# Attention into a gated feed-forward layer on one core: three early gate/value blocks, casts in another place, merged squares, and two output tiles moved forward

## The chip, the core and the metric

The kernel runs on one core of a Trainium2 chip. The core has TensorE (PE: matmuls, and PEld: its weight loads), VectorE (DVE), ScalarE (ACT), GpSimd (POOL) and SyncE (SP), each with an instruction stream of its own that it works through in order. DMA transfers are issued from SP's and GpSimd's streams and run on 16 shared DMA engines. The metric is the device time of one execution in microseconds; lower is better.

## What is computed

```python
# q, k, v: 8 batches, 12 heads, 448 rows, 64 columns
scores = q @ k.T / sqrt(64)
attn   = max(scores, 0) ** 2 / 448
x      = attn @ v                      # -> 3584 tokens x 768
xn     = x / sqrt(mean(x * x) + 1e-6) * rms_g
g, val = xn @ w_gate, xn @ w_val       # 768 -> 1536
out    = (g * sigmoid(g) * val) @ w_out    # 1536 -> 768
```

Inputs and output are float32; the kernel works in bfloat16 with float32 sums.

## The kernel before

The work is done batch by batch, with the tokens of a batch (448) along the free axis. A head pair j (0 to 5) fills 128 partitions; the six pairs of a batch are the six slices of 128 of the 768 model columns.

**Attention** of batch b (lines 136 to 241). For batches 0 and 1 TensorE transposes q and k (`pe_transposes`, L142) and VectorE copies the result out (`qkT`, L148). From batch 2 on VectorE reorders q and k (`kqp`, L155) and a DMA transposes them (`kqT`, L166). `scores` (L187) makes score tiles psS for two of four chunks of rows at a time; there are two buffers of psS. The relu leaves psS by ScalarE (L196) or, for the chunks named by `dve_chunks`, by VectorE (L194). `squares` (L202) multiplies r by itself on VectorE, one instruction for each chunk. `attend` (L209) multiplies by v into psAV, of which there is one buffer. ScalarE writes xT from it (L220), and VectorE x*x, `x2` (L221).

**Norm.** `norm_stat` sums x2 over the columns with a matrix of ones (psSS, L251), ScalarE takes the root (L258), VectorE the reciprocal (L262, rstd). `norm_apply` forms xn = xT * g * rstd in six VectorE instructions (L268).

**Feed-forward.** `gate` and `value` make one block of 128 of the 1536 hidden columns each: twelve matmuls into psG or psV (L251; each is one half of 64 output partitions). ScalarE takes the silu of psG (L289), VectorE multiplies it with psV into hT (L295). `outproj` makes an output tile of 128 tokens in two parts, 512 and 256 wide (psO, L251), which ScalarE (L312) and VectorE (L314) copy out; a DMA from SP stores them (L321). psG, psV, psO, psSS and psT share three buffers, `mm`.

**Weights** are loaded in 18 slices of float32 by DMAs from SP into seven staging buffers (`fetch_w`, L115), and GpSimd casts each to bfloat16 (`cast_w`, L125). The first fetch waits for batch 0's last load of k. q, k and v are loaded by GpSimd's casting DMAs (`load`, L95); q and k have one buffer, v has two.

**The order** is fixed by hand: instructions stand in each engine's stream as the program emits them. `spread` takes a main list of units with costs (gate/value blocks, output tiles) and places other units (attention of the next batch, its norm, preparations) at shares of the main cost. In the prologue, batch 0's attention runs alone, with filler matmuls (`warm`, L368) between its units, then its norm, fourteen fillers, and xn. Then gate/value 0 runs; attention 1 begins at 0.45 of it, and what is left of attention 1 stands alone behind it, then the norm of batch 1. The loop over b from 1 (L440) has as its main list gate/value b and out tiles: all seven tiles of batches 0 and 1 at b = 1, three tiles at each even b, four at each odd one from 3 on. Beside it stand attention b + 1, then its `norm_stat` at 0.86 and `norm_apply` at 0.90 of the main cost.

## Time and profile before

| | us |
|---|---|
| median of three runs | 517.49 (513.65 to 518.02) |
| the profiled execution, its own time | 515.89 |
| its span, first to last instruction | 514.10 |
| TensorE busy in the span | 476.3 (93%), mean granted clock 0.963 |
| VectorE busy | 301.0 (59%) |
| ScalarE busy | 256.2 (50%) |
| GpSimd busy | 53.8 (10%) |

All times in the rows below are microseconds from the span's start unless marked ns. A matmul's busy time contains a latency that the next one overlaps, so a unit's cost on TensorE is read as the distance between starts. "Granted clock" is the share of TensorE's full 2.4 GHz; its two levels are 1.2 and 2.4 GHz. The wait in brackets behind an instruction is the idle time of its engine ahead of it and what ended it.

### The profile page before, as it was taken

How to read it: one execution, taken by the hardware profiler on the slowest of the kernel's cores; microseconds unless marked ns; L12 is line 12 of the kernel's file. 1: busy time of each engine (PE TensorE's matmuls, PEld its weight loads, DVE VectorE, ACT ScalarE, POOL GpSimd, SP SyncE). 2: the span in 40 equal slices, each digit the busy share in tenths (PEclk: the TensorE clock that was granted, in tenths of full speed). 3: DMA queues.
4: the chain of work that ended last, by engine and by line, in shares of the span. 5: the costliest groups of instructions: out<-in, count | busy, mean ns of one | idle time of the engine just before them, and what ended most of it. 6: DMA issues, size and time to landing. Idle time of an engine off the chain costs nothing.

```text
span 514.1 us, 10918 instructions
## 1 busy us (share of the span) xinstructions
PE 476.3 (93%) x4754; PEld 264.8 (52%) x4754; DVE 301.0 (59%) x489; ACT 256.2 (50%) x367; POOL 53.8 (10%) x53
## 2 busy tenths in 40 slices
PE   6966899769799999999999999999999999999996
PEld 2322465327545554456554645465555645466774
DVE  2996458953285467576566476756567466545210
ACT  3652146632366466655666466636655556642210
POOL 5283540200200000010001000020000000000000
PEclk8887799959999999999999999999999999999999
DMA  9999920660999751099105930296005210012013
GB/s 116 288 319 258 337 111 2 79 83 1 139 203 132 144 108 34 1 161 171 32 2 92 220 84 1 48 191 124 2 9 108 68 50 1 1 33 62 1 32 93
DMA packets 81712, 50.65 MB, mean 99 GB/s; under 512 B 35072, under 2 KB 76544, under 8 KB 81664
## 3 DMA queue, kind: packets, MB, share of 16 engines
q1 hardware_dynamic: 48944, 33.43, 25.9%
q0 software_dynamic: 32720, 16.52, 25.1%
q8 instruction: 37, 0.61, 0.5%
q14 instruction: 11, 0.09, 0.1%
HBM read 47.19 MB, written 11.01 MB: 113 GB/s over the span
## 4 chain that ended last, share of the span: by engine, by line
PE 76%; DVE 14%; issue 5%; ACT 3%; DMA 1%; POOL 0%; DVEq 0%; ACTq 0%; POOLq 0%
PE psV L251 22%; PE psG L251 22%; PE psO L251 16%; PE psS L187 8%; PE psAV L209 6%; DVE xn L268 5%; DVE r L202 5%; DVE rstd L262 2%; PE psSS L251 2%; DVE r L194 1%; ACT r L196 1%; DMA kb<-in_k_dram 1%; PE psT L142 1%; PE psW L368 1%; ACT xT L220 1%
## 5 line engine op out<-in xcount | busy, mean ns | idle before, releaser
L196 ACT ACTIVATE r<-psS 112x896 bf16<-112x896 f32 x162 | 140.6, 915 | 39.7 <-PE psS L187 39.4
L251 PE MATMUL psG<-xn,wg_sb 128*64 128x448 bf16 x1152 | 136.6, 360 | 13.5 <-DVE xn L268 13.3
L251 PE MATMUL psV<-xn,wv_sb 128*64 128x448 bf16 x1152 | 128.3, 357 | 0.0
L295 DVE TENSOR_TENSOR hT<-sil,psV 128x448 bf16<-128x448 bf16 x96 | 59.6, 621 | 104.0 <-PE psV L251 102.3
L202 DVE TENSOR_TENSOR r<-r 112x896 bf16<-112x896 bf16 x192 | 117.9, 657 | 0.0
L251 PE MATMUL psO<-wo_sb,hT 128*64 128x512 bf16 (+1 forms) x1344 | 115.4, 326 | 0.0
L289 ACT ACTIVATE sil<-psG 128x448 bf16<-128x448 f32 x96 | 52.2, 544 | 104.5 <-PE psG L251 103.2
L251 PEld LDWEIGHTS <-wg_sb 128*64 128x64 bf16 x1152 | 67.8, 110 | 70.1 <-issue 34.9
L251 PEld LDWEIGHTS <-hT 128*64 128x64 bf16 x1344 | 77.9, 110 | 33.6 <-issue 4.0
L251 PEld LDWEIGHTS <-wv_sb 128*64 128x64 bf16 x1152 | 67.5, 111 | 47.2 <-issue 12.8
L209 PE MATMUL psAV<-r,vb 112*64 112x448 bf16 x384 | 49.6, 362 | 7.5 <-DVE r L202 6.5
L220 ACT ACTIVATE xT<-psAV 128x448 bf16<-128x448 f32 x48 | 26.1, 543 | 43.0 <-PE psAV L209 42.6
L312 ACT COPY ost<-psO 128x512 f32<-128x512 f32 x28 | 16.4, 585 | 60.5 <-PE psO L251 56.0
L187 PE MATMUL psS<-kqT 64*128 64x448 bf16 x288 | 40.8, 354 | 3.0 <-ACT r L196 1.5
L221 DVE TENSOR_TENSOR x<-xT 128x448 bf16<-128x448 bf16 x48 | 19.2, 401 | 40.5 <-ACT xT L220 40.4
L262 DVE RECIPROCAL rstd<-rstd 128x448 f32<-128x448 f32 x8 | 23.6, 2953 | 31.7 <-ACT rstd L258 31.7
L209 PEld LDWEIGHTS <-vb 112*64 112x64 bf16 x384 | 22.6, 110 | 28.9 <-issue 13.3
L194 DVE TENSOR_SCALAR r<-psS 112x896 bf16<-112x896 f32 x30 | 32.6, 1086 | 7.1 <-PE psS L187 7.1
L95 POOL DMA_DIRECT2D qb<-in_q_dram x10 | 8.8, 880 | 213.1 <-DVE x L221 135.6
L268 DVE SCALAR_TENSOR_TENSOR xn<-xT,g_sb,rstd 128x448 bf16<-128x448 bf16 x48 | 30.4, 702 | 0.1
L187 PEld LDWEIGHTS <-kqT 64*128 64x128 bf16 x288 | 8.8, 94 | 28.6 <-issue 28.5
L187 PE MATMUL psS<-qkT 64*128 64x448 bf16 x96 | 16.4, 392 | 5.6 <-ACT r L196 3.3
(33 smaller groups left out, 166.3 us busy)
## 6 DMA issues: line engine op xcount, KB each, us to landing
qb<-in_q_dram POOLq DMA_DIRECT2D x7, 672.0 KB, 9.8
kb<-in_k_dram POOLq DMA_DIRECT2D x7, 672.0 KB, 14.8
vb<-in_v_dram POOLq DMA_DIRECT2D x7, 672.0 KB, 10.0
wst<-in_moe_w_gate_dram SPq DMA_DIRECT2D x6, 768.0 KB, 10.7
wst<-in_moe_w_val_dram SPq DMA_DIRECT2D x6, 768.0 KB, 11.7
wst<-in_moe_w_out_dram SPq DMA_DIRECT2D x6, 768.0 KB, 15.8
out_dram<-ost SPq DMA_DIRECT2D x8, 336.0 KB, 3.7
out_dram<-ost SPq DMA_DIRECT2D x8, 288.0 KB, 2.7
```

The costliest lines, as they stand in the source:

```text
L187: nc.tensor.matmul(out=psS[:, hh, :S], lhsT=flat[:, o : o + P], rhs=rhs, start=True, stop=True)
L194: nc.vector.tensor_relu(out=r[:], in_=psS[:PC, :, :S])
L196: nc.scalar.activation(out=r[:], in_=psS[:PC, :, :S], func=ACT.Relu)
L202: nc.vector.tensor_tensor(out=r[:], in0=r[:], in1=r[:], op=ALU.mult)
L209: nc.tensor.matmul(out=psAV[hh * D : (hh + 1) * D, :], lhsT=ld["v", b][:, 2 * j + hh, c * D : (c + 1) * D], rhs=rsq[b, j, c][:, hh, :], st ...
L220: nc.scalar.mul(out=xT[:, j, :], in_=psAV[:], mul=inv_attn)
L221: nc.vector.tensor_tensor(out=x2s[b][:, j, :], in0=xT[:, j, :], in1=xT[:, j, :], op=ALU.mult)
L251: nc.tensor.matmul(out=ps[prt, :w], lhsT=lhsT[:, prt], rhs=rhs, start=start, stop=stop)
L262: nc.vector.reciprocal(out=rstd[:], in_=rstd[:])
L268: nc.vector.scalar_tensor_tensor(out=xn[:, kt, :], in0=xTs[b][:, kt, :], scalar=g_sb[:, kt : kt + 1], in1=rstds[b][:], op0=ALU.mult, op1=A ...
L289: nc.scalar.activation(out=s[:], in_=psG[:], func=ACT.Silu)
L295: nc.vector.tensor_tensor(out=hTs[b // 2][:, fb, o : o + S], in0=sil.pop((b, fb))[:], in1=psV[:], op=ALU.mult)
```

## The change

- **Early blocks.** For batch 0, the gate and value products of hidden blocks 0, 1 and 2 are made from xT, which now holds x*g, without the norm (`early_matmuls`). When rstd is there, VectorE multiplies both products by it as they leave PSUM, and silu and product follow (`early_rest`). Block 0 stands ahead of psSS and blocks 1 and 2 behind it. Blocks 0 and 1 lie in the two psS buffers, block 2 in psAV's and one of `mm`. The fourteen fillers go.
- **g moves.** `leave` multiplies by g and the attention's scale when ScalarE reads psAV; `norm_apply` is a plain product. x*x is now made by ScalarE from psAV.
- **Merged squares.** One tile r holds both chunks of a step, one VectorE instruction squares them; the last pair of batch 0 is split between ScalarE and VectorE. The first two qkT copies of batch 1 go to ScalarE.
- **Attention's order.** `attend` and `leave` come later behind their scores (`lag`).
- **Weights.** The first four slices (two of gate, two of value) are loaded by GpSimd's casting DMAs straight into bfloat16. Fourteen are staged in six buffers; the first of these fetches waits for the last casting DMA. The first two casts stand behind batch 1's loads, which are now in halves and ahead of the early blocks; the other twelve wait for the scaled block 1 of batch 0.
- **Places.** Two output tiles stand behind gate/value 0, five are left at b = 1. Attention 1 is spread over 0.08 to 0.68 of that list, its norm stands at 0.74 and 0.80 of it. In later batches the attention ends at 0.74 instead of 0.80, and the norm stands at 0.80 and 0.84 instead of 0.86 and 0.90. Batch 2's loads and preparation move forward.

The diff, cut to its core:

```diff
-        nc.gpsimd.tensor_copy(out=dst, in_=src)
+        return eng.tensor_copy(out=dst, in_=src)
...
     def scores(b, j, cs, on_dve):
...
-        for c, psS in zip(cs, pss):
-            r = apool.tile([PC, 2, S], BF16, name="r", tag="r")
+        r = apool.tile([PC, len(cs), 2, S], BF16, name="r", tag="r")
...
     def squares(b, j, cs, split=False):
+        r = raw.pop((b, j, cs[0]))
+        if split:
+            nc.scalar.activation(out=r[:, 0], in_=r[:, 0], func=ACT.Square)
+            nc.vector.tensor_tensor(out=r[:, 1], in0=r[:, 1], in1=r[:, 1], op=ALU.mult)
+        else:
             nc.vector.tensor_tensor(out=r[:], in0=r[:], in1=r[:], op=ALU.mult)
...
-        nc.scalar.mul(out=xT[:, j, :], in_=psAV[:], mul=inv_attn)
-        nc.vector.tensor_tensor(out=x2s[b][:, j, :], in0=xT[:, j, :], in1=xT[:, j, :], op=ALU.mult)
+    def leave(b, j):
+        psAV = psAVs.pop((b, j))
+        nc.scalar.mul(out=xTs[b][:, j, :], in_=psAV[:], mul=ga_sb[:, j : j + 1])
+        nc.scalar.activation(
+            out=x2s[b][:, j, :], in_=psAV[:], func=ACT.Square, scale=inv_attn
+        )
...
-            nc.vector.scalar_tensor_tensor(
-                out=xn[:, kt, :], in0=xTs[b][:, kt, :], scalar=g_sb[:, kt : kt + 1],
-                in1=rstds[b][:], op0=ALU.mult, op1=ALU.mult,
+            nc.vector.tensor_tensor(
+                out=xn[:, kt, :], in0=xTs[b][:, kt, :], in1=rstds[b][:], op=ALU.mult
             )
...
+    def early_rest(b, fb, parts):
+        t = late["early"].tile([P, 2, S], FP32, name="gv", tag="gv")
+        for part in range(2):
+            nc.vector.tensor_tensor(
+                out=t[:, part, :], in0=parts[part][:, :S], in1=rstds[b][:], op=ALU.mult
+            )
+        s = spool.tile([P, S], BF16, name="sil", tag="sil")
+        nc.scalar.activation(out=s[:], in_=t[:, 0, :], func=ACT.Silu)
+        hT, o = hidden(b)
+        return nc.vector.tensor_tensor(
+            out=hT[:, fb, o : o + S], in0=s[:], in1=t[:, 1, :], op=ALU.mult
+        )
...
+        for which, s in order[:NCAST]:
+            w, w_sb = ((moe_w_gate, wg_sb) if which == "g" else (moe_w_val, wv_sb))
+            last = nc.gpsimd.dma_start(
+                out=w_sb[:, :, s * FS : (s + 1) * FS],
+                in_=w.rearrange("(kt p) f -> p kt f", p=P)[:, :, s * FS : (s + 1) * FS],
+            )
+        order = order[NCAST:]
         first = fetch_w(*order[0])
+        hold(first, last, "fetches follow what the first batch needs")
...
-        norm_stat(0)
-        warm(14)
-        norm_apply(0)
+        early_matmuls(0, 0, blocks[0])
+        norm_stat(0)
+        psE = ps_a.tile([P, S], FP32, name="psE", tag="ps_a")
+        blocks.append((psE[:], ps_m.tile([P, 512], FP32, name="psE", tag="mm")[:]))
+        early_matmuls(0, 1, blocks[1])
+        early_matmuls(0, 2, blocks[2])
+        ahead(2)
+        norm_apply(0)
+        early_rest(0, 2, blocks[2])
...
+                if fed[0] == 2:
+                    hold(i, held[0], "casts on Pool follow the norm of the first batch")
...
-        for fn in spread(main, [(0.45, 1.3, attention(1, True, lambda j: (3,)))]):
+        main = [(c, stepped(n, f)) for n, (c, f) in enumerate(gate_value(0, 3) + out_tiles(0, 0, 2))]
+        spans = [(0.02, 0.06, [lambda: rest_of(0), lambda: rest_of(1)])]
+        spans.append((0.08, 0.68, pending))
...
-            spans.append((0.0, 0.80, attention(b + 1, False, lambda j: (3,) if j % 2 else ())))
+            spans.append((0.0, 0.74, attention(b + 1, False, lambda j: (3,) if j % 2 else (), True)))
         if b + 1 < B:
-            spans.append((0.86, 0.9, [lambda b=b: norm_stat(b + 1)]))
-            spans.append((0.90, 0.95, [lambda b=b: norm_apply(b + 1)]))
+            spans.append((0.80, 0.82, [lambda b=b: norm_stat(b + 1)]))
+            spans.append((0.84, 0.86, [lambda b=b: norm_apply(b + 1)]))
```

How this moves instructions is shown at three places. First, VectorE at the norm of batch 0. Before (r are squares, x_274 is x*x, then reciprocal, xn, the products into hT):

```order
L221 TENSOR_TENSOR x_274<-xT 128x448
L202 TENSOR_TENSOR r<-r 112x896 x2
L221 TENSOR_TENSOR x_274<-xT 128x448
L262 RECIPROCAL rstd<-rstd 128x448
L268 SCALAR_TENSOR_TENSOR xn<-xT,g_sb,rstd 128x448 x6
L295 TENSOR_TENSOR hT<-sil,psV 128x448 x5
```

VectorE at the same place now (psE is an early block in PSUM, gv the scaled block):

```order
L216 TENSOR_TENSOR r<-r 112x1792
L214 TENSOR_TENSOR r<-r 112x896
L297 RECIPROCAL rstd<-rstd 128x448
L303 TENSOR_TENSOR xn<-xT,rstd 128x448 x6
L328 TENSOR_TENSOR gv<-psE,rstd 128x448 x2
L334 TENSOR_TENSOR hT<-sil,gv 128x448
```

The products x*x are gone from VectorE, the squares are merged, and three scaled blocks (the last two rows stand there three times in a row) come behind xn.

Second, GpSimd at the end of batch 0's loads. Before (wst is a staged slice):

```order
L95 DMA qb<-in_q_dram 112x6x256
L95 DMA kb<-in_k_dram 112x6x256
L95 DMA vb<-in_v_dram 112x6x256
L125 CAST wg_sb<-wst 128x6x256
L125 CAST wv_sb<-wst 128x6x256
```

GpSimd at the same place now:

```order
L100 DMA vb<-in_v_dram 112x6x256
L454 DMA wg_sb<-in_moe_w_gate_dram 128x6x256
L454 DMA wv_sb<-in_moe_w_val_dram 128x6x256
...
L100 DMA qb<-in_q_dram 112x6x256
L100 DMA kb<-in_k_dram 112x6x256
...
L133 CAST wg_sb<-wst 128x6x256
L133 CAST wv_sb<-wst 128x6x256
```

Casting DMAs of four slices and six loads of batch 1 now stand ahead of the first cast.

Third, VectorE at the norm of batch 1. Before:

```order
L202 TENSOR_TENSOR r<-r 112x896 x2
L221 TENSOR_TENSOR x_954<-xT 128x448
L262 RECIPROCAL rstd<-rstd 128x448
L268 SCALAR_TENSOR_TENSOR xn<-xT,g_sb,rstd 128x448 x6
L295 TENSOR_TENSOR hT<-sil,psV 128x448 x6
```

VectorE at the same place now (ost is an output tile, kqp the reordered k of batch 2):

```order
L216 TENSOR_TENSOR r<-r 112x1792
L355 TENSOR_TENSOR hT<-sil,psV 128x448
L297 RECIPROCAL rstd<-rstd 128x448
L303 TENSOR_TENSOR xn<-xT,rstd 128x448 x6
L374 COPY ost<-psO 128x256 x2
L166 COPY kqp<-kb 112x6x4x64
```

The last block of gate/value 0 now stands between the attention of batch 1 and its norm, and the copies of two output tiles and the preparation of batch 2 follow xn.

## Rows read from the trace of the kernel before

**Rows 1.** Stretches: length, busy time (and count) of each engine, clock, DMA share, GB/s

```profile
92.70:114.20 21.50, 13.82 (x92) 5.30 (x90) 17.60 (x28) 10.42 (x14) 2.79 (x3) 0.70 0.74 97
187.00:465.00 278.00, 272.89 (x2800) 148.78 (x2797) 174.73 (x296) 162.13 (x232) 8.38 (x9) 1.00 0.37 68
```

**Rows 2.** Timeline, TensorE, around the first norm: start, length, operation, count, wait

```profile
42.14 1.12 PE L209 MATMUL psAV<-r,vb 112*64 112x448 bf16 x4 [0.25 <-DVE r L202]
...
56.03 2.50 PE L251 MATMUL psV<-xn,wv_sb 128*64 128x448 bf16 x12
```

**Rows 3.** Timeline, VectorE, first attention (last row: a pair of squares in the second)

```profile
11.48 1.09 DVE L194 TENSOR_SCALAR r<-psS 112x896 bf16<-112x896 f32 x1 [1.10 <-PE psS L187]
...
14.97 0.62 DVE L148 COPY qkT<-psT 128x896 bf16<-128x896 bf16 x1 [0.26 <-PE psT L142]
...
19.46 0.62 DVE L148 COPY qkT<-psT 128x896 bf16<-128x896 bf16 x1
...
97.31 1.15 DVE L202 TENSOR_TENSOR r<-r 112x896 bf16<-112x896 bf16 x2
```

**Rows 4.** Timeline, a square on VectorE and two casts on GpSimd beside it

```profile
34.25 3.29 DVE L202 TENSOR_TENSOR r<-r 112x896 bf16<-112x896 bf16 x1
...
33.77 1.88 POOL L125 CAST wv_sb<-wst 128x1536 bf16<-128x1536 f32 x1
35.60 1.46 POOL L125 CAST wg_sb<-wst 128x1536 bf16<-128x1536 f32 x1
```

**Rows 5.** Timeline, TensorE: units whose starts follow each other without a wait

```profile
71.73 0.39 PE L142 MATMUL psT<-ident,kb 112*64 112x112 bf16 x8
...
72.15 1.30 PE L251 MATMUL psG<-xn,wg_sb 128*64 128x448 bf16 x12
73.39 0.55 PE L187 MATMUL psS<-qkT 64*128 64x448 bf16 x4
...
119.07 1.32 PE L251 MATMUL psV<-xn,wv_sb 128*64 128x448 bf16 x12
120.20 1.32 PE L251 MATMUL psG<-xn,wg_sb 128*64 128x448 bf16 x12
...
148.84 0.93 PE L209 MATMUL psAV<-r,vb 112*64 112x448 bf16 x8
149.70 0.55 PE L187 MATMUL psS<-kqT 64*128 64x448 bf16 x4
150.18 1.50 PE L251 MATMUL psO<-wo_sb,hT 128*64 128x256 bf16 x24
...
493.53 15.79 PE L251 MATMUL psO<-wo_sb,hT 128*64 128x512 bf16 x192
```

**Rows 6.** Timeline, TensorE and VectorE, at the boundary to batch 2

```profile
180.33 1.33 PE L251 MATMUL psSS<-x,ones_bf 128*64 128x448 bf16 x12
...
186.16 3.67 DVE L268 SCALAR_TENSOR_TENSOR xn<-xT,g_sb,rstd 128x448 bf16<-128x448 bf16 x6
...
187.28 0.59 PE L251 MATMUL psG<-xn,wg_sb 128*64 128x448 bf16 x4
...
190.19 0.55 PE L187 MATMUL psS<-kqT 64*128 64x448 bf16 x4
```

**Rows 7.** Groups by line: count, busy us, mean ns of one, idle before

```profile
L196 ACT ACTIVATE r<-psS 112x896 bf16<-112x896 f32 x162 | 140.6, 915 | 39.7 <-PE psS L187 39.4
L220 ACT ACTIVATE xT<-psAV 128x448 bf16<-128x448 f32 x48 | 26.1, 543 | 43.0 <-PE psAV L209 42.6
L262 DVE RECIPROCAL rstd<-rstd 128x448 f32<-128x448 f32 x8 | 23.6, 2953 | 31.7 <-ACT rstd L258 31.7
```

**Rows 8.** Loads: first fetch (SP), a cast and its wait (GpSimd), landing of q, k, v

```profile
15.30 0.40 SPq L115 DMA_DIRECT2D wst<-in_moe_w_gate_dram  x1
...
47.70 1.47 POOL L125 CAST wv_sb<-wst 128x1536 bf16<-128x1536 f32 x1 [3.14 <-DMA wst<-in_moe_w_val_dram]
...
DMA to landing us min/median/max: 3.0/9.8/31.9
```

More of the change, by code (lines that the diff above doesn't have):

```diff
@@ L91, in alloc_ld, with fetch @@
         ld["v", b] = ldpool.tile([PC, H, NCH * D], BF16, name="vb", tag="vb", bufs=2)
+    def fetch(b):
+        alloc_ld(b)
+        for nm in ("q", "k", "v"):
+            load(nm, b)
     def load(nm, b, h0=0, h1=H):
@@ L115, in fetch_w, with cast_w @@
         return nc.sync.dma_start(out=dst, in_=src)
-    def cast_w(which, s):
+    def cast_w(which, s, eng=None):
+        eng = eng or nc.gpsimd
         st = stage.pop((which, s))
@@ L124, in cast_w @@
             dst = {"g": wg_sb, "v": wv_sb}[which][:, :, s * FS : (s + 1) * FS]
-        nc.gpsimd.tensor_copy(out=dst, in_=src)
+        if eng is nc.scalar:
+            return nc.scalar.copy(out=dst, in_=src)
+        return eng.tensor_copy(out=dst, in_=src)
     xTs, x2s = {}, {}
@@ L131 @@
     rsq = {}
-    raw = {}
+    raw, psAVs = {}, {}
     HH = H // 2
@@ L147, in pe_transposes @@
         t = late["qkT"].tile([P, 2, S], BF16, name="qkT", tag="qkT")
-        nc.vector.tensor_copy(out=t[:], in_=psT[:])
+        if b == 1 and j < 2:
+            nc.scalar.copy(out=t[:], in_=psT[:])
+        else:
+            nc.vector.tensor_copy(out=t[:], in_=psT[:])
         qkT[b, j] = t
@@ L267, in norm_apply, with hidden, early_matmuls @@
         for kt in range(KT):
-            nc.vector.scalar_tensor_tensor(
-                out=xn[:, kt, :], in0=xTs[b][:, kt, :], scalar=g_sb[:, kt : kt + 1],
-                in1=rstds[b][:], op0=ALU.mult, op1=ALU.mult,
+            nc.vector.tensor_tensor(
+                out=xn[:, kt, :], in0=xTs[b][:, kt, :], in1=rstds[b][:], op=ALU.mult
             )
         xns[b] = xn
+    def hidden(b):
         i = b // 2
-        if b % 2 == 0:
+        if i not in hTs:
             hp = hpool if i % 2 == 0 else late["hpool"]
             hTs[i] = hp.tile([P, FT, 2 * S], BF16, name="hT", tag="hT")
+        return hTs[i], (b % 2) * S
+    def early_matmuls(b, fb, parts):
+        for part, w_sb in enumerate((wg_sb, wv_sb)):
+            for kt in range(KT):
+                halves(
+                    parts[part], S, w_sb[:, kt, fb * P : (fb + 1) * P], xTs[b][:, kt, :],
+                    kt == 0, kt == KT - 1,
+                )
[11 more added lines that the diff above has]
+        )
     def project(w_sb, b, fb, nm):
@@ L324, in outproj, with gate_value @@
                 g += n
-    def gate_value(b):
+    def gate_value(b, f0=0):
         units = []
-        for fb in range(FT):
+        for fb in range(f0, FT):
             units.append((1.13, lambda fb=fb: gate(b, fb)))
@@ L356 @@
     nc.sync.dma_start(out=g_sb[:], in_=moe_rms_g.rearrange("(kt p) -> p kt", p=P))
+    ga_sb = wpool.tile([P, KT], FP32, name="ga_sb", tag="rmsga")
+    nc.vector.tensor_scalar_mul(out=ga_sb[:], in0=g_sb[:], scalar1=inv_attn)
     load("q", 0, 2, 6)
@@ L364, in warm, with hold @@
     def warm(n):
-        ps = ps_a.tile([P, S], FP32, name="psW", tag="ps_a")
+        ps = ps_m.tile([P, S], FP32, name="psW", tag="mm")
         for _ in range(n):
             nc.tensor.matmul(out=ps[:], lhsT=warm_in[:, :P], rhs=warm_in[:], start=True, stop=True)
-    def name_of(i):
-        return (i.ins if hasattr(i, "ins") else i)
-    with tc.tile_pool(name="stage", bufs=7) as sp, tc.tile_pool(name="qkT", bufs=2) as tp:
-        late["stage"], late["qkT"] = sp, tp
+    def hold(i, until, reason):
+        i, until = (x.ins if hasattr(x, "ins") else x for x in (i, until))
+        tc.add_manual_dep(
+            i,
+            until.name,
+            mybir.DependencyInfo(mybir.DependencyClass.Sync, mybir.DependencyReason.DATA),
+            reason=reason,
+        )
+    NST = 6
+    with tc.tile_pool(name="stage", bufs=NST) as sp, tc.tile_pool(name="qkT", bufs=2) as tp, tc.tile_pool(
+        name="early", bufs=2
+    ) as ep:
+        late["stage"], late["qkT"], late["early"] = sp, tp, ep
         order = []
@@ L392 @@
                 warm(2)
-        norm_stat(0)
-        warm(14)
-        norm_apply(0)
+        alloc_ld(1)
+        for h0 in (0, HH):
+            for nm in ("q", "k", "v"):
+                load(nm, 1, h0, h0 + HH)
         fed = [0]
@@ L431, in prepare @@
         dma_transposes(b, half)
-    def fetch(b):
-        alloc_ld(b)
-        for nm in ("q", "k", "v"):
-            load(nm, b)
-    fetch(2)
     full = S // P
```

104 lines of the change are left out of this document (59 added, 45 removed).

## The prediction

> **What bounds the kernel now.** I read the table of stretches first. From 187 us to 465 us TensorE is busy 272.89 of 278.00 us at a granted clock of 1.00, the upper level of 2.4 GHz: nothing but fewer matmuls would help there. Around the second norm (92.70 to 114.20) the clock is 0.70 on average and TensorE is busy 13.82 of 21.50 us [rows 1]. So the time to win lies ahead of 187 us.
>
> Next, TensorE's timeline: the attention of batch 0 ends at 42.14 + 1.12 = 43.26 us, and the second product of gate/value 0 starts only at 56.03, and its twelve matmuls take 2.50 us [rows 2]. Then the time of one unit when nothing is in the way, as the distance from one start to the next [rows 5]: a gate or value block 120.20 - 119.07 = 1.13 us, the sixteen transposes of a head pair 72.15 - 71.73 = 0.42, one psS step 150.18 - 149.70 = 0.48, one psAV 149.70 - 148.84 = 0.86, an out tile 15.6 / 4 = 3.9 (the last 192 matmuls, less 0.2 of latency).
>
> With these I count the work from 43.26 to the first gate of batch 2 at 187.28 [rows 6]: 48 gate and value blocks 54.5; three psSS 3.4 (as many matmuls as a block); six transposes 2.5; two attentions (24 psS, 12 psAV) 21.8; seven out tiles 27.3; one psS of the next batch 0.5. Sum 110.0. The stretch took 144.0, so **34.0 us are lost** in it, and the 43.26 ahead of it are themselves mostly waiting. Last, each batch boundary: the gate starts at 187.28 and is through at 190.19, when psS follows, 2.9 for 1.13 of work: 1.8 lost because six xn products (3.67) still run [rows 6].
>
> **The first attention.** Its pace is VectorE's. Between two copies of qkT lie 19.46 - 14.97 = 4.49 us, with 0.62 for the copy and 1.09 for the relu [rows 3]. Later a square that is half of a 1.15 us pair in the quiet [rows 3] takes 3.29, from 34.25 to 37.54, across two casts on GpSimd that run from 33.77 to 37.06 [rows 4]: 1.36 us for each cast. The change takes the x*x product to ScalarE, merges two squares into one, and removes the casts from this stretch: four weight slices now come as casting DMAs, the next two casts stand behind batch 1's loads, the other twelve behind the norm. VectorE's round becomes copy 0.54 (0.08 of each operation overlaps the next) + relu 1.00 + two merged squares. A merged square isn't in the trace; it lies between 0.9 and the pair's 1.15; I take 1.08. Sum 3.7. ScalarE's round: three relus of 0.9 and two readings of psAV at 0.54 [rows 7], 3.7 as well. The relu of head pair 0 ends at 11.48 + 1.09 = 12.57 [rows 3]. From there four rounds of 3.7 and one of 3.2 (no copy) bring pair 5's relu to 30.6, with its squares, the release of psAV and the last psAV 33.5. Six loads of batch 1 are now issued on GpSimd in this stretch, and a cast may fall on the last squares: 0 to 4 more, I take 1. **The attention ends at 34.5 instead of 43.26: 8.8 won** (5.8 to 9.8).
>
> The Trainium skill ("SBUF — State Buffer", Who interferes with whom) says that a VectorE instruction with two SBUF inputs contends with a GpSimd instruction that reads SBUF, and that the later one fully blocks. The trace agrees: the square on record ends 0.48 us after the second cast, 1.36 us late for each of the two. By that rule each of the twelve casts still to come can cost a square that it meets its whole 1.46 us [rows 4].
>
> **The norm of batch 0.** Call the end of the attention t. Before, only 14 filler matmuls lay between psSS and the first gate. Now block 0 stands ahead of psSS, blocks 1 and 2 behind it. The clock had fallen there before (2.50 us for twelve matmuls where 1.3 is usual [rows 2, 5]), so I let block 0 and psSS take 5.4 instead of 3.4. psSS ends at t + 5.8. Root and reciprocal took 186.16 - 181.46 = 4.7 at a boundary [rows 6], a table load included that isn't needed here; the reciprocal alone is 2.95 [rows 7]; I take 3.7, to t + 9.5; blocks 1 and 2 and a transpose end at t + 10.8. Six xn products at 0.6 (3.67 for six [rows 6]; the new form has one operand fewer, 0.40 to 0.70) end at t + 13.1, and gate/value 3 at t + 14.5. Now comes a new wait: the scores of batch 1 need the two psS buffers that hold blocks 0 and 1 until VectorE has scaled them. VectorE does block 2 first (three products, 1.8), then 0 and 1. None of these products is in the trace; at xn's 0.6 each the second buffer is free at t + 17.9. TensorE reaches t + 18.3 with 11.2 us of work done: **7.1 lost** (5 to 9). Behind the waiting psS stand gate 4 and all that follows.
>
> **Gate/value 0 with attention 1.** 17.0 of blocks and 12.6 of attention, 29.6 for TensorE. VectorE needs 3.7 a round for six rounds, which end 22 us after t + 18.5 if left alone. The held casts run right here: twelve at 0 to 1.36 are 0 to 16 us, where about 7 are free. ScalarE has 3.5 relus, two psAV readings and 1.7 silu a round, 4.9 of the 5.0 that TensorE leaves. I take **5.0 lost** (0 to 11).
>
> **The end of gate/value 0.** The norm of batch 1 has two out tiles beside it instead of nothing. Behind psSS stand one 256-wide part and one whole tile, 5.3 us; the chain from psSS to the last xn took 186.16 + 3.67 - 181.46 = 8.4 at a boundary [rows 6], and the copy of a 256-wide part now stands behind xn in VectorE's queue. **3.1 lost** (2 to 4). Another 2.5 (1.8 to 4) for the change between psS and block matmuls (a block behind a psS takes 1.24 where 72.15 starts one [rows 5], not 1.13), and the first psS of batch 2. Batch 2's kqp copies stand in VectorE's queue right after: its loads are issued when the last cast is through (twelve from 52.5 us on at 1.5 to 1.9 each: about 75 us), some 20 us ahead of their use at 34.5 + 60; hidden, unless they land as late as batch 1's v did, 31.9 us after issue [rows 8].
>
> **Six boundaries.** psSS moves to 0.80 of the main work: two out tiles, 7.8, lie behind it instead of 5.3. The chain of 8.4 is nearly covered, but a 256-wide copy behind xn holds a bank. 1.3 of the 1.8 go: **7.8 won** (4 to 10). The other side: 0.54 of ScalarE for each of 48 x*x [rows 7], 26 us in all, beside TensorE in the later batches; attention in 0.74 of the main work instead of 0.80. I charge **1.5** (0 to 4).
>
> **The sum** is made against the profiled execution, 515.9 us (span 514.1 and 1.8 around it), 1.6 below the median of the runs, 517.5. Stalls now 7.1 + 5.0 + 3.1 + 2.5 = 17.7 against 34.0: 16.3 won. 8.8 + 16.3 + 7.8 - 1.5 = 31.4, which gives **484.5 us**.
>
> **The rivals.**
> (a) Everything hides: attention ends at 33.5 (9.8 won), stalls 5 + 0 + 3.1 + 1.8 = 9.9 (24.1 won), boundaries 1.7 each (10.2). 44.1 in all: 472. For it: VectorE's own work leaves 7 us for the casts. Against: ScalarE is full at the same time.
> (b) The casts are not held back but moved onto attention 1's squares: 12 at 1.36 is 16.3, 9 over what is free, and with a cast on the first attention's tail and a missed kqp copy 3 + 2 more beyond what I counted: 484.5 + 4 + 5 = 494. By the Trainium skill's rule above ("SBUF — State Buffer", Who interferes with whom) it would be 12 x 0.10 = 1.2 us more. For it: both engines have that work in the same 25 us. Against: most of VectorE's other work reads PSUM, and casts can slip in beside it.
> (c) The data come late. Before, the fetches start when 1680 KB of the first batch (as written, in bfloat16) have landed, at 15.30 [rows 8]: 120 KB a us. Behind these now stand the last v and four slices, 1872 KB, to 31 us; only then fetches and batch 1 share the DMA engines, at 1.47 + 3.14 = 4.6 us a slice [rows 8]. Batch 1's first q and k halves then land at about 41; TensorE wants them at t + 10.4 = 45. Should they take as long as the v, to 55, TensorE waits 10: 494.5.
> (d) Slower than before: the clock. If the waits at t + 15 to t + 18 drop TensorE to 1.2 GHz and VectorE-paced work never lets it recover until the norm of batch 1, the 40 us of work in gate/value 0 cost 40 more: 524.5. It decides from 38 us of such work on. For it: 0.70 in the second row of [rows 1]. Against: that row has TensorE busy for 64%, while this stretch would have over 80%.
>
> **How the numbers follow.** Forecast 0.50, (a) 0.17, (b) 0.18, (c) 0.10, (d) 0.03, and 0.02 for a gain that is lost in several small ways and ends near zero. A measurement of this kernel can tell about 1%, 5.2 us, from no change. Faster by more: 0.95, within 0.02, slower 0.03. The range reaches from (a) to a little past (b) and (c): 472 to 499.
>
> **What would show it.** Right: copies of qkT 3.7 us apart in the first attention and psAV's end at 33 to 37 us; psSS of batch 0 between two early blocks and the reciprocal hidden beside them; a wait of psS for VectorE's product on psE; squares of 1.1 that stretch to 2 or 3 beside casts at 52 to 75; gates at the boundaries at 1.2 to 1.6. Wrong: qkT copies still 4.5 apart; early blocks that wait for a DMA; a granted clock of 0.5 beyond 60 us; waits of psS for ScalarE in the later batches.

## The result, and the profile after

| | before | after |
|---|---|---|
| median of four runs each, us | 516.98 (513.65 to 518.02) | 487.12 (486.24 to 488.83) |
| ratio, 95% interval | | 0.9435 (0.9392 to 0.9478) |
| profiled execution, its span | 515.89, 514.1 | 487.15, 485.4 |
| mean granted clock | 0.963 | 0.987 |

The forecast was 484.5 us, range 472 to 499. The change brings 28.7 us of span. Medians and ratios below leave out executions that were disturbed as a whole; the profiles of experiments 4 and 8 (494.58 and 498.80 us) are of such executions, so only single stretches of them are compared.

The table of stretches of after (columns as in [rows 1]), cut near the end of the first attention, the first score of batch 1, the first output tile, gate/value 1 and batch 2:

```profile
37.00:53.00 16.00, 12.80 (x133) 7.10 (x134) 11.20 (x16) 6.36 (x11) 0.00 (x0) 1.00 1.24 258
53.00:90.00 37.00, 33.96 (x366) 18.00 (x364) 27.59 (x28) 27.97 (x42) 24.92 (x15) 0.95 0.89 224
90.00:102.00 12.00, 11.22 (x123) 7.43 (x120) 7.39 (x10) 4.62 (x7) 0.00 (x0) 1.00 0.10 14
166.00:320.00 154.00, 152.80 (x1570) 85.97 (x1570) 88.76 (x116) 100.18 (x152) 8.40 (x9) 1.00 0.50 83
```

The stretch around the second norm, 0.70 of the clock and 64% busy in [rows 1], is now 94% busy (11.22 of 12.00) at 1.00, and from 166 to 320 us TensorE is busy 152.80 of 154.00. TensorE's timeline of after, at the points by which the prediction reckons:

```profile
35.44 1.21 PE L224 MATMUL psAV<-r,vb 112*64 112x448 bf16 x8 [1.31 <-ACT x L240]
...
48.79 1.32 PE L286 MATMUL psV<-xn,wv_sb 128*64 128x448 bf16 x12 [0.69 <-DVE gv L328]
50.59 0.37 PE L198 MATMUL psS<-qkT 64*128 64x448 bf16 x2 [0.48 <-DVE gv L328]
...
52.39 0.37 PE L198 MATMUL psS<-qkT 64*128 64x448 bf16 x2 [1.44 <-DVE gv L328]
52.69 1.92 PE L286 MATMUL psG<-xn,wg_sb 128*64 128x448 bf16 x12
...
89.81 2.78 PE L286 MATMUL psO<-wo_sb,hT 128*64 128x512 bf16 x24
...
98.86 0.38 PE L286 MATMUL psG<-xn,wg_sb 128*64 128x448 bf16 x2
...
101.88 1.33 PE L286 MATMUL psV<-xn,wv_sb 128*64 128x448 bf16 x12
...
115.84 0.55 PE L198 MATMUL psS<-kqT 64*128 64x448 bf16 x4 [1.28 <-issue]
...
142.69 0.95 PE L224 MATMUL psAV<-r,vb 112*64 112x448 bf16 x8 [1.16 <-ACT x L240]
...
149.79 0.95 PE L224 MATMUL psAV<-r,vb 112*64 112x448 bf16 x8 [1.65 <-ACT x L240]
...
166.10 1.33 PE L286 MATMUL psG<-xn,wg_sb 128*64 128x448 bf16 x12
```

The attention of batch 0 ends at t = 35.44 + 1.21 = 36.65 (43.26 in [rows 2]). The gate of batch 2 starts at 166.10 (187.28 in [rows 6]), one whole block without a wait. Between the two lie 129.45 us for the same 110.0 of work that the prediction counts: 19.5 lost, 34.0 before. So the 28.7 us are 6.6 ahead of t, 14.5 from t to 166.10, and 7.5 behind (319.3 us to the span's end instead of 326.8). The new wait is there too: three waits for VectorE's scaled blocks (gv), 0.69, 0.48 and 1.44.

VectorE's timeline of after: three copies of qkT, the last relu and the last half square of the first attention, the six xn, then squares in gate/value 0, beside casts (58.37 to 74.58) and without (last):

```profile
14.88 0.62 DVE L159 COPY qkT<-psT 128x896 bf16<-128x896 bf16 x1 [0.40 <-PE psT L150]
...
18.75 0.62 DVE L159 COPY qkT<-psT 128x896 bf16<-128x896 bf16 x1
...
23.12 0.62 DVE L159 COPY qkT<-psT 128x896 bf16<-128x896 bf16 x1 [0.42 <-PE psT L150]
...
32.14 1.09 DVE L205 TENSOR_SCALAR r<-psS 112x896 bf16<-112x896 f32 x1 [0.93 <-PE psS L198]
...
34.34 1.88 DVE L214 TENSOR_TENSOR r<-r 112x896 bf16<-112x896 bf16 x1
...
44.36 3.30 DVE L303 TENSOR_TENSOR xn<-xT,rstd 128x448 bf16<-128x448 bf16 x6
...
58.37 3.74 DVE L216 TENSOR_TENSOR r<-r 112x1792 bf16<-112x1792 bf16 x2
...
63.56 2.22 DVE L216 TENSOR_TENSOR r<-r 112x1792 bf16<-112x1792 bf16 x1
...
66.24 1.81 DVE L216 TENSOR_TENSOR r<-r 112x1792 bf16<-112x1792 bf16 x1
...
69.04 3.55 DVE L216 TENSOR_TENSOR r<-r 112x1792 bf16<-112x1792 bf16 x2
...
74.58 1.69 DVE L216 TENSOR_TENSOR r<-r 112x1792 bf16<-112x1792 bf16 x1
...
81.87 1.08 DVE L216 TENSOR_TENSOR r<-r 112x1792 bf16<-112x1792 bf16 x1
```

GpSimd's timeline of after, the casts beside these squares:

```profile
34.08 1.67 POOL L133 CAST wv_sb<-wst 128x1536 bf16<-128x1536 f32 x1 [0.61 <-DMA wst<-in_moe_w_val_dram]
53.20 1.47 POOL L133 CAST wg_sb<-wst 128x1536 bf16<-128x1536 f32 x1 [17.45 <-DVE hT L334]
...
58.84 2.33 POOL L133 CAST wg_sb<-wst 128x1536 bf16<-128x1536 f32 x1
61.11 2.32 POOL L133 CAST wv_sb<-wst 128x1536 bf16<-128x1536 f32 x1
```

A merged square is 1.08 alone, as taken. Beside casts a pair of them takes 3.55 to 3.74 instead of 2.08, and the cast beside it 2.33 instead of 1.47: each stretches the other.

ScalarE's two readings of psAV in after, grouped by line; the first answers to L220 in [rows 7]:

```profile
L239 ACT ACTIVATE xT<-psAV,ga_sb 128x448 bf16<-128x448 f32 x48 | 30.5, 636 | 7.9 <-PE psAV L224 7.9
L240 ACT ACTIVATE x<-psAV 128x448 bf16<-128x448 f32 x48 | 26.3, 549 | 0.0
```

### The profile page after: what moved, and what is told of

Same layout as the page of the kernel before. It is cut to its first block, busy times and chain, and to the rows that moved or that the text cites. A ratio compares the mean times of both kernels' runs of the same rounds, so it can differ in the third digit from the quotient of the medians.

```text
span 485.4 us, 10790 instructions
## 1 busy us (share of the span) xinstructions
PE 459.6 (95%) x4744; PEld 266.9 (55%) x4744; DVE 271.3 (56%) x347; ACT 280.7 (58%) x421; POOL 56.5 (12%) x56
## 4 chain that ended last, share of the span: by engine, by line
PE 63%; ACT 6%; issue 1%; DVE 0%; DVEq 0%
PE psO L286 20%; PE psG L286 16%; PE psV L286 15%; PE psAV L224 6%; PE psS L198 5%; ACT r L207 4%; PE psSS L286 1%; ACT sil L349 1%; ACT xT L239 0%; ACT x L240 0%; ACT ost L372 0%; DVE ost L374 0%; DVEq L374 0%
## 5 line engine op out<-in xcount | busy, mean ns | idle before, releaser
L286 PE MATMUL psG<-xn,wg_sb 128*64 128x448 bf16 x1116 | 125.1, 356 | 1.4 <-DVE xn L303 1.2
L286 PE MATMUL psV<-xn,wv_sb 128*64 128x448 bf16 x1116 | 122.6, 354 | 0.7 <-DVE gv L328 0.7
L216 DVE TENSOR_TENSOR r<-r 112x1792 bf16<-112x1792 bf16 x95 | 107.8, 1145 | 2.7 <-ACT r L207 2.7
L286 PEld LDWEIGHTS <-hT 128*64 128x64 bf16 x1344 | 83.4, 110 | 28.5 <-issue 0.7
L224 PE MATMUL psAV<-r,vb 112*64 112x448 bf16 x384 | 45.2, 354 | 6.1 <-ACT x L240 5.2
L374 DVE COPY ost<-psO 128x256 f32<-128x256 f32 x28 | 11.7, 421 | 48.7 <-PE psO L286 48.4
L239 ACT ACTIVATE xT<-psAV,ga_sb 128x448 bf16<-128x448 f32 x48 | 30.5, 636 | 7.9 <-PE psAV L224 7.9
L205 DVE TENSOR_SCALAR r<-psS 112x896 bf16<-112x896 f32 x27 | 29.4, 1088 | 5.4 <-PE psS L198 5.3
L303 DVE TENSOR_TENSOR xn<-xT,rstd 128x448 bf16<-128x448 bf16 x48 | 26.4, 619 | 0.2
L240 ACT ACTIVATE x<-psAV 128x448 bf16<-128x448 f32 x48 | 26.3, 549 | 0.0
## 6 DMA issues: line engine op xcount, KB each, us to landing
kb<-in_k_dram POOLq DMA_DIRECT2D x6, 672.0 KB, 14.5
```

The costliest lines, as they stand in the source:

```text
L205: nc.vector.tensor_relu(out=r[:, i], in_=psS[:PC, :, :S])
L216: nc.vector.tensor_tensor(out=r[:], in0=r[:], in1=r[:], op=ALU.mult)
L224: nc.tensor.matmul(out=psAV[hh * D : (hh + 1) * D, :], lhsT=ld["v", b][:, 2 * j + hh, c * D : (c + 1) * D], rhs=rsq[b, j, c][:, hh, :], st ...
L239: nc.scalar.mul(out=xTs[b][:, j, :], in_=psAV[:], mul=ga_sb[:, j : j + 1])
L240: nc.scalar.activation(out=x2s[b][:, j, :], in_=psAV[:], func=ACT.Square, scale=inv_attn)
L286: nc.tensor.matmul(out=ps[prt, :w], lhsT=lhsT[:, prt], rhs=rhs, start=start, stop=stop)
```

## The experiments

A "+" time compares medians with after's 487.12, or spans with its 485.4. Each ratio is to before, measured beside it; only in experiments 2, 3 and 7 does its interval lie clear of after's (0.9392 to 0.9478), so a "+" elsewhere is not told from nothing by the times alone.

**1. Without the early blocks.** The order of before at the first norm, inside the new kernel:

```diff
-        early_matmuls(0, 0, blocks[0])
         norm_stat(0)
-        early_matmuls(0, 1, blocks[1])
-        early_matmuls(0, 2, blocks[2])
+        warm(14)
...
-        main = [(c, stepped(n, f)) for n, (c, f) in enumerate(gate_value(0, 3) + out_tiles(0, 0, 2))]
+        main = [(c, stepped(n, f)) for n, (c, f) in enumerate(gate_value(0) + out_tiles(0, 0, 2))]
```

> The changed kernel without the early blocks: psSS, 14 filler matmuls, xn, then all twelve blocks of gate/value 0 as before; all else as changed. Theory: the early blocks fill the wait behind psSS, but delay the norm by block 0 and give VectorE nine more products on which psS waits. From the end of the first attention the changed kernel lost 4.9 us up to its first psS; without the blocks the chain root 0.7 + reciprocal 2.95 + xn 3.3 + first gate leaves 6.3 lost. So only 1 to 3 us slower than 487.1, that is 488 to 490. Rival: the early blocks carry the gain at this norm (before lost 12.6 us there), and without them it comes back: 494 or more.

Measured: 489.06, ratio 0.9467 (0.9405 to 0.9529), against after's 0.9435 (0.9392 to 0.9478): the intervals overlap. In the profile the first output tile starts 56.5 us after t (37.0 to 93.51) instead of 53.2, so 3.3 us are lost there. The clock falls again; TensorE at the second product:

```profile
47.62 2.50 PE L286 MATMUL psV<-xn,wv_sb 128*64 128x448 bf16 x12
```

It takes the 2.50 of [rows 2], twice the usual 1.3, and psSS ahead of it 2.45. The edit has two side effects that the cut above does not show: attention 1 and the norm of batch 1 are placed anew, and the held casts wait for xn instead of a scaled block, so they begin at 47.30 instead of 53.20. The early blocks, by far the longest part of the diff, are worth at most some 2 to 3 us of the 30.

**2. The norms of the later batches back at their old place.**

```diff
-            spans.append((0.80, 0.82, [lambda b=b: norm_stat(b + 1)]))
-            spans.append((0.84, 0.86, [lambda b=b: norm_apply(b + 1)]))
+            spans.append((0.86, 0.9, [lambda b=b: norm_stat(b + 1)]))
+            spans.append((0.90, 0.95, [lambda b=b: norm_apply(b + 1)]))
```

> The changed kernel with the norms of batches 2 to 7 back at 0.86 and 0.90 of the main work; all else as changed. Theory: the boundary stall was the chain psSS to xn (8.0 us now) against one and a half out tiles (5.3 us); moved back, each of six boundaries loses about 1.3 to 1.5 again: 8 to 9 us slower, 495 to 496. Rival: the boundaries are shorter because x*x has left VectorE and xn is cheaper (3.3 instead of 3.67); then at most 0.4 for each comes back: 487 to 489.5.

Measured: 496.67, ratio 0.9610 (0.9533 to 0.9686); +9.6, and +9.4 of span (494.8). TensorE's timeline of this kernel, at the first psS of batch 2 and at the boundary to batch 2:

```profile
116.22 0.56 PE L198 MATMUL psS<-kqT 64*128 64x448 bf16 x4 [2.04 <-issue]
...
161.95 5.41 PE L286 MATMUL psO<-wo_sb,hT 128*64 128x256 bf16 x72
...
167.77 0.61 PE L286 MATMUL psG<-xn,wg_sb 128*64 128x448 bf16 x4
168.54 0.38 PE L286 MATMUL psG<-xn,wg_sb 128*64 128x448 bf16 x2 [0.16 <-DVE xn L303]
...
170.46 0.55 PE L198 MATMUL psS<-kqT 64*128 64x448 bf16 x4
```

Only 5.4 us of output tiles lie behind psSS, the gate waits for one xn after the other, and psS follows 170.46 - 167.77 = 2.69 after its start. In after 9.3 us lie behind psSS, and psS follows 1.26 after the gate's start. Not all of the 9.4 is the norm's place: from the gate of batch 2 to the end this kernel takes 494.8 - 167.77 = 327.0 and after 319.3, which is 7.7. The other 1.7 lie ahead of the gate, where psS of batch 2 waits 2.04 instead of 1.28 and two blocks behind it take 1.87 and 1.99 (clock 0.72 from 116 to 122). Moving two lines by six hundredths is still the largest single gain that was isolated.

**3. No output tiles ahead of gate/value 1.** All seven stand at b = 1 again:

```diff
-        main = [(c, stepped(n, f)) for n, (c, f) in enumerate(gate_value(0, 3) + out_tiles(0, 0, 2))]
+        main = [(c, stepped(n, f)) for n, (c, f) in enumerate(gate_value(0, 3))]
...
-            main += out_tiles(0, 2, NT)
+            main += out_tiles(0, 0, NT)
```

> The changed kernel with all seven out tiles at b = 1 again, attention 1 over the same blocks of gate/value 0 and the norm of batch 1 alone behind them; all else as changed. Theory: psSS to the first gate of batch 1 then has nothing beside it: 8.0 + 1.1 instead of the 1.9 us lost now, so 6 us slower, 493, and a lower clock there. Rival: the seven tiles only change their place, and what the norm loses is regained where attention 2 has five tiles beside it now and seven then (6.1 us lost at b = 1 in the changed kernel): within 2 us of 487.

Measured: 491.95, ratio 0.9544 (0.9489 to 0.9598); +4.8, span +5.6. TensorE behind psSS of batch 1:

```profile
96.34 3.26 PE L286 MATMUL psG<-xn,wg_sb 128*64 128x448 bf16 x12 [4.48 <-DVE xn L303]
```

The norm's chain shows as a wait of 4.48, and the block behind it takes 3.26 instead of the usual 1.33 (clock 0.50 from 95 to 100). All of the 5.6 lies ahead of the gate of batch 2, which starts at 171.70; behind it the kernel takes the same 319.3 as after.

**4. The first four slices staged and cast** on GpSimd as before, instead of casting DMAs; batch 1's loads stand behind their casts.

```diff
-        for which, s in order[:NCAST]:
...
-            last = nc.gpsimd.dma_start(
...
-        hold(first, last, "fetches follow what the first batch needs")
+        hold(first, last_k, "fetches follow what the first batch needs")
```

> The changed kernel with the first four weight slices staged and cast on GpSimd again, ahead of batch 1's loads, fetches from the last k on; all else as changed. Theory: four casts fall on the squares of the first attention, up to 1.36 us each of which some is slack (VectorE idles 0.3 to 0.9 us a round): the first attention ends 2 to 5 us later than 36.65, the run 489 to 492. Rival: the first attention is paced by the chain of psS, relus and psAV's one buffer, not by VectorE, and four casts change it by less than 1 us: 486.5 to 488.

Measured: 486.75, ratio 0.9435 (0.9383 to 0.9488): the same as after, the time that the rival gives; its reason is not shown by this. The profile has squares stretched in the first attention again, which takes 26.0 us from the end of pair 0's relu instead of after's 24.2 (12.48 to 36.65). But kernels whose first attention is after's own take 22.9 (experiment 9) to 25.8 (experiment 12), as the first two casts miss or meet the last squares, so casting DMAs are worth nothing here that can be told.

**5. Casts not held back.**

```diff
-                    hold(i, held[0], "casts on Pool follow the norm of the first batch")
...
-        ahead(2)
+        ahead(14)
```

> The changed kernel without the hold: all fourteen casts run as their slices land. Theory (a cast and a VectorE instruction with two SBUF inputs exclude each other): the gate and value casts leave attention 1 and meet xn and the early products instead; squares in attention 1 were stretched by 5.6 us in all, six of twelve casts leave them, while xn grows by 1 to 3 us on the path to the first gate: 486 to 490, with xn of batch 0 at 4.5 us or more instead of 3.30. Rival: the casts' place does not matter because the DMA paces them: xn stays 3.3 and the run 487.

Measured: 490.46, ratio 0.9488 (0.9430 to 0.9545); +3.3. Staged slices arrive one by one from 37 to 60 us, xn takes 4.57 instead of 3.30 as the theory said, the first gate waits 1.05 for it, and the last six casts still fall on squares (61 to 74). But the profiled execution, 7.9 us of span longer than after's, is only 2.3 behind after at the first output tile (92.08); most of the rest comes where psS of batch 2 waits 5.34 for its transposes, against 1.28. The hold is worth 0 to 3 us; the run does not separate it from that wait.

**6. w_out by six casting DMAs** behind batch 1's loads, so that six casts go:

```diff
+        order = [w for w in order if w[0] != "o"]
+        for s in range(FT // 2):
+            nc.gpsimd.dma_start(out=wo_sb[:, 2 * s : 2 * s + 2, :], in_=...)
```

> The changed kernel with w_out loaded by six casting DMAs behind batch 1's loads instead of six staged slices and casts; all else as changed. Theory: the last six casts (63 to 75 us) stretch the squares of attention 1 by some 3.9 us; without them VectorE keeps up and gate/value 0 loses 2 to 4 us less: 483 to 485. Rival 1: the loss in gate/value 0 (6.6 us) comes from the clock and the buffers of psS and qkT, not from casts: 486.5 to 488. Rival 2: the casting DMAs share the engines with the staged slices and make these late, gates wait for weights: 490 or more.

Measured: 487.31 in two executions, ratio 0.9414 (0.9373 to 0.9455): no difference that can be told. GpSimd's timeline of this kernel (two rows), and VectorE's:

```profile
42.17 0.70 POOL L474 DMA_DIRECT2D wo_sb<-in_moe_w_out_dram  x1 [4.25 <-DMA vb<-in_v_dram]
...
47.03 1.48 POOL L133 CAST wg_sb<-wst 128x1536 bf16<-128x1536 f32 x1
```

```profile
32.30 0.62 DVE L214 TENSOR_TENSOR r<-r 112x896 bf16<-112x896 bf16 x1
...
46.73 3.67 DVE L334 TENSOR_TENSOR hT<-sil,gv 128x448 bf16<-128x448 bf16 x1
```

GpSimd's later DMA issues each wait until an earlier load has landed, the first two casts come out at 47 to 50 us instead of 32 to 36, one early product takes 3.67 instead of 0.63, and the first psS is through 19.2 us after t instead of 16.0. In exchange the first attention, now without a cast on its tail, ends 22.9 us behind pair 0's relu (24.2 in after), and the stretch to the first output tile is 35.7 instead of 37.1. So two casts cost after 1.3 us in the first attention; experiment 9's kernel, where they come late enough to miss its last squares, takes 22.9 there too. In gate/value 0 the squares that stretched by 5.6 us in after stretch by 0.8 here, and the stretch is only 1.4 shorter, at a clock of 0.94 (0.95 in after): as rival 1 says, most of the 6.6 lost there stays without the stretched squares.

**7. Two squares per step** instead of the merged one:

```diff
-            nc.vector.tensor_tensor(out=r[:], in0=r[:], in1=r[:], op=ALU.mult)
+            for i in range(len(cs)):
+                nc.vector.tensor_tensor(out=r[:, i], in0=r[:, i], in1=r[:, i], op=ALU.mult)
```

> The changed kernel with two square instructions of 896 for each merged one; all else as changed. Theory: a pair costs 1.15 in the quiet and a merged one 1.08, 0.07 more in each of 12 steps of the first attention, and only where VectorE paces it: 0 to 1 us slower, 487 to 488. Rival: merging is what shortened the round (4.49 to 4.0): the first attention would be 2 us or more longer, 489.5.

Measured: 493.36, ratio 0.9528 (0.9490 to 0.9567); +6.2. VectorE and GpSimd of this kernel:

```profile
57.78 6.57 DVE L217 TENSOR_TENSOR r<-r 112x896 bf16<-112x896 bf16 x4
```

```profile
60.23 1.85 POOL L133 CAST wg_sb<-wst 128x1536 bf16<-128x1536 f32 x1
62.03 1.85 POOL L133 CAST wv_sb<-wst 128x1536 bf16<-128x1536 f32 x1
```

Four half squares take 6.57 where after's two merged ones take 3.74 for the same data: while casts follow each other, one VectorE square comes through per cast here, the half as well as the merged one (62.03 - 60.23 = 1.80 from cast to cast here, 61.11 - 58.84 = 2.27 there). A copy of qkT behind them makes psS wait 3.07, and the first output tile starts 57.1 after t instead of 53.2. By VectorE's own time merging saves 0.07 a pair (1.15 against 1.08); in this kernel it is worth 4.3 us of span and 6.2 of the medians, more than theory and rival had, 3.9 of it from t to the first output tile.

**8. x\*x back on VectorE.**

```diff
-        nc.scalar.activation(out=x2s[b][:, j, :], in_=psAV[:], func=ACT.Square, scale=inv_attn)
+        nc.vector.tensor_tensor(out=x2s[b][:, j, :], in0=xT[:, j, :], in1=xT[:, j, :], op=ALU.mult)
```

It sums the squares of x\*g, not of x. 

> The changed kernel with x*x made by VectorE from xT again (so the norm sums the squares of x*g instead of x); all else as changed. Theory 1: x*x on VectorE costs a round of the first attention 0.3 us, in all 2 us there, and gains 0.5 us wherever psAV waits for ScalarE's second reading (5.2 us of waits in five places): 485 to 489. Theory 2, from the prediction: VectorE paces the first attention, so its round grows by the full 0.39 and the run is 2 to 3 us slower, 489 to 490. Rival: ScalarE's second reading is the price of the change in the later batches (26 us of ScalarE): 2 us or more faster, below 485.

Measured: 491.24, ratio 0.9487 (0.9442 to 0.9532); +4.1. VectorE in the first attention of this kernel, then TensorE at batch 2's attention:

```profile
21.19 0.39 DVE L241 TENSOR_TENSOR x<-xT 128x448 bf16<-128x448 bf16 x1 [1.85 <-ACT xT L239]
```

```profile
156.16 0.95 PE L224 MATMUL psAV<-r,vb 112*64 112x448 bf16 x8 [0.73 <-ACT xT L239]
...
162.83 0.95 PE L224 MATMUL psAV<-r,vb 112*64 112x448 bf16 x8 [1.22 <-ACT xT L239]
```

The product itself is 0.39. What costs is the wait in front of it: VectorE stands 1.85, then 1.20 and 0.93, for ScalarE's xT with the next squares behind it, and the first attention takes 29.2 from pair 0's relu instead of 24.2. From the gate of batch 2 on the kernel is 1.4 shorter than after (497.0 - 179.10 = 317.9 for 319.3): that is what the second reading on ScalarE costs there, net of the product on VectorE. In this profile psS of batch 2 also waits 4.93, against 1.28, so the time of the run does not show x\*x alone.

**9. Batch 3's loads later at b = 1.**

```diff
-            prep = [lambda: prepare(2, 0), lambda: prepare(2, 1), lambda: fetch(3)]
-            spans.append((0.0, 0.1, prep))
+            prep = [lambda: prepare(2, 0), lambda: prepare(2, 1)]
+            spans.append((0.0, 0.067, prep))
+            spans.append((0.3, 0.3, [lambda: fetch(3)]))
```

> The changed kernel with batch 3's loads at 0.3 of the work at b = 1 instead of 0.067; all else as changed. Theory: the first psS of batch 2 waits for its transposing DMA (1.28 us in the changed kernel, 0.6 to 5.3 us in the other runs), because batch 3's loads are issued a microsecond behind that DMA and share its engines; issued later, the transpose lands sooner and the wait is gone: 1 to 3 us faster than 487.1, with less spread, 484 to 486. Rival: the wait is the late kqp copy behind xn on VectorE; then the wait stays and the run is 487.

Measured: 490.11, ratio 0.9499 (0.9446 to 0.9552); +3.0. The edit missed: GpSimd has nothing else in its queue there, so the loads go out when the buffers of q and k are free, at 101.63, beside the transposes at 101.74. The theory was not tested by it; the last section says what the runs together show of it.

**10 and 11. Two edits alone in the kernel before**: x\*x on ScalarE, and merged squares.

```diff
-        nc.vector.tensor_tensor(out=x2s[b][:, j, :], in0=xT[:, j, :], in1=xT[:, j, :], op=ALU.mult)
+        nc.scalar.activation(out=x2s[b][:, j, :], in_=psAV[:], func=ACT.Square, scale=inv_attn)
```

> The kernel before with x*x made by ScalarE from psAV, and nothing else of the change. Theory: in the first attention VectorE waits in its own order for ScalarE's xT ahead of each x*x, and so loses more than the product's 0.39 us; freed of it the first attention ends 3 to 5 us ahead of 43.26 and the end of attention 1 (93 to 104 us) 1 to 2 us sooner: 511 to 513. Rival: with psAV held until ScalarE's second reading, and ScalarE the fuller engine, the gain is given back: 515 to 518.

```diff
-        for c in cs:
-            r = raw.pop((b, j, c))
-            nc.vector.tensor_tensor(out=r[:], in0=r[:], in1=r[:], op=ALU.mult)
-            rsq[b, j, c] = r
+        r = raw.pop((b, j, cs[0]))
+        nc.vector.tensor_tensor(out=r[:], in0=r[:], in1=r[:], op=ALU.mult)
+        for i, c in enumerate(cs):
+            rsq[b, j, c] = r[:, i]
```

> The kernel before with two squares merged into one instruction, and nothing else of the change. Theory: beside casts VectorE gets one instruction in between two casts, and a merged square does twice the work in it; in the first attention eight casts cost two squares 3.6 to 4.1 us instead of 1.15 at the worst, so merging ends it 2 to 4 us ahead of 43.26: 513 to 515. Rival: merging saves only the 0.07 us of a pair that the quiet shows, 0.9 us in the first attention: 516 to 517.

Measured: ratio 1.0040 (0.9999 to 1.0081) for x\*x, 0.9970 (0.9934 to 1.0005) for the merged squares. Neither is told from no change, both theories missed, and neither brings what it is worth in the new kernel (4.1 and 6.2 by the medians). VectorE of experiment 10, beside casts:

```profile
32.50 6.16 DVE L202 TENSOR_TENSOR r<-r 112x896 bf16<-112x896 bf16 x4
```

With x\*x gone these four squares take 6.16, against 2.22 at 16.83 where no cast runs, and the attention ends at 43.56 (43.26 before). As long as casts run there, what is taken off VectorE is filled by waiting for GpSimd: in the kernel before, the same step with x\*x in it takes 5.43 (33.40 to the next relu at 38.83), here 6.08. From pair 0's relu the first attention takes 30.7 before, 31.0 with x\*x moved alone, 30.5 with squares merged alone, 24.2 in after, and 29.2 in after with x\*x put back. So it is shortened by the edits together, not by one.

**12. The six scalings ahead of the three products** (and experiment 9's edit, again without effect on the loads):

```diff
-        early_rest(0, 2, blocks[2])
+        early_scale(0, 2, blocks[2])
...
-        spans = [(0.02, 0.06, [lambda: rest_of(0), lambda: rest_of(1)])]
+        spans = [(0.02, 0.06, [scales, prods])]
```

> The changed kernel with batch 3's loads at 0.3 and the six scalings of the early blocks ahead of their three products into hT. Theory: psS waits for the last scaling, which ends 1.1 us sooner when two products stand behind it: the first psS of batch 1 is through at 15 us after the first attention's end instead of 16, and with the loads later the run is 2 to 4 us faster than the changed kernel: 483 to 485. Rival: gates of gate/value 0 then wait for buffers or VectorE is paced by casts and squares all the same: as with the later loads alone.

Measured: 486.82, ratio 0.9430 (0.9378 to 0.9482): not told from after. VectorE of this kernel:

```profile
49.19 3.28 DVE L330 TENSOR_TENSOR gv<-psE,rstd 128x448 f32<-128x448 f32 x6
```

All score buffers are free after 3.28 us, the wait of 1.44 is gone (0.69 and 0.50 stay), and the first output tile starts 50.4 us after t instead of 53.2 (51.8 in experiment 9, which has the same places but after's order of products). The span, 483.8, is the shortest profiled, but what is won there is near the spread of a run.

## Why the prediction was right, step by step

**The first attention: 8.8 forecast, 6.6 measured.** The pace was forecast at 3.7 a round and came out at 4.1 in the mean (18.75 - 14.88 = 3.87, then 4.37 and 4.02), from 4.49. So pair 5's relu ends at 32.14 + 1.09 = 33.23 instead of 30.6, more than the whole miss; what follows it takes 3.4, forecast 3.9. VectorE's own round is 3.6, but VectorE alone does not pace the stretch, as the prediction took: in each round it also waits for TensorE's scores or transposes, 0.24 to 0.93 at a time. One of ScalarE's terms was small: the readings of psAV were put at 0.54 each, but xT now takes 636 ns. Its scale is a tile with one value per partition, and that adds 93 ns to the 543 of [rows 7]. The Trainium skill ("ScalarE: Activation LUTs", What ACT_TABLE_LOAD costs, the paragraph on the rate of ACTIVATE) gives some 93 ns for each such operand; the rows agree. Behind pair 5's relu, psAV's one buffer is held for 636 + 549 ns, and the last psAV waits 1.31 for ScalarE. Casts fell on the last squares (1.88 for a half that is 0.62 in experiment 6), 1.3 us, where 1 was taken.

**The contention** goes by the Trainium skill's rule ("SBUF — State Buffer", Who interferes with whom) again: the half square from 34.34 ends at 36.22, 0.47 us after the cast does (34.08 + 1.67). The rule also says that the later one of the two waits, whichever it is; the casts of 2.33 agree.

**The norm of batch 0: 7.1 forecast, 4.9 lost.** The first psS of batch 1 that waited is through at 52.69, 16.0 after t, not 18.3. The blocks ran at the full clock (1.30 each), where 2.0 had been added for a fall, and the new xn took 3.30 for six. The mechanism, psS behind the scaled blocks, is the one predicted. The clock fell behind it instead (1.92 for the block at 52.69; 0.95 in the mean to 90).

**Gate/value 0: 5.0 forecast, 6.6 lost** (37.1 for 30.5 of work). Its squares stretch by 5.6 us in all: 3.74 + 2.22 + 1.81 + 3.55 + 1.69 = 13.01, for two pairs of 2.08 and three of 1.08, together 7.4. That is rival (b)'s contention at a third of its price of 16.3: three casts and most of a fourth are through ahead of the first square, and a merged square meets one cast where two halves meet two (experiment 7). But little of the loss follows from it: experiment 6, with 0.8 of stretch, still loses 5.2. What the rest is made of no run takes apart; the clock (0.95) and waits for qkT and psS are there. (The prediction counts 17.0 of blocks here; the sixteen that are left are 18.1. The sum does not use it.)

**The end of gate/value 0: 3.1 forecast, 1.9 lost** (101.88 - 98.86 = 3.0 for 1.13). **The rest to batch 2: 2.5 forecast, 6.1 lost.** This is the step that was sized worst: it was costed as switches alone. It holds three waits that the text did not price: 1.28 for the transposes of batch 2 (the profile calls it "issue" here; in experiments 4 and 6 it names their DMA at the same place), and 1.16 and 1.65 for psAV. That ScalarE now reads psAV twice is the smaller part of these two: in experiment 8, where it reads once, the same two waits are 0.73 and 1.22. The rest is ScalarE's order, in which the reading stands behind the copy of an output tile that TensorE has yet to make (the copy starts at 141.09 after a wait of 1.18, xT at 141.57). "Waits of psS for ScalarE in the later batches" was named as a sign of error; the wait is psAV's.

**Boundaries and later batches: 7.8 - 1.5 = 6.3 forecast, 7.5 measured.** Behind the gate of batch 2, experiment 2 puts the norm's place at 7.7, for 7.8, and experiment 8 ScalarE's second reading at 1.4, for 1.5 (in the old order the same move wins 1.3 there: 516.3 - 190.80 = 325.5 in experiment 10, 326.8 before). The 1.2 beyond these (the cheaper xn and the merged squares are candidates) no run assigns.

**The sum**: 6.6 + 14.5 + 7.5 = 28.6, forecast 31.4. That it came so close is partly luck: the six terms are off by 2.2, 2.2, 1.6, 1.2, 3.6 and 1.2, 12.0 in all, and all but 2.8 cancels. No rival took over. (c) did not come: no block waits for a weight, and the waits at 50 us name VectorE. (d) did not: the clock is 0.95 in gate/value 0.

By experiment, the parts are worth 9.6 (place of the norms; 7.7 without the wait ahead of batch 2), 6.2 (merged squares; 4.3 of span) and 4.8 (tiles; 5.6 of span). Not told from nothing by their times are x\*x (4.1, with 5.0 in the first attention of its profile), the early blocks (0 to 3), the hold (0 to 3) and the casting DMAs (nothing). They do not add up: the squares and x\*x are worth this only in the new order. The later `attend` and `leave`, the copies of qkT on ScalarE and the earlier preparation of batch 2 were not taken out in any run.

## What to carry to other kernels

Read how much independent work stands behind the start of a latency chain (here psSS, root, reciprocal, xn: 8.4 us) and move the chain, not the work: it was the cheapest edit and the largest gain. Where two engines take turns at a resource, count instructions, not only their time: merging two saved 0.07 of VectorE's time a pair and some 4 to 6 us of the run. An edit that wins nothing alone may still be needed for the others, so test it by taking it out of the final version as well.
